# Reordering VectorE's queue around the seam of two Strassen-like stages: an earlier turn of x, earlier sums for C21, and an output addition split by columns

## The chip, the cores and the metric

The kernel runs on one core of a Trainium2 chip. The metric is the device time of one execution in microseconds. The median of three timed runs of the kernel before is 930.23 us (929.91 to 932.08); the profiled execution spans 927.9 us.

## The reference

Shapes are q, k, v: (8, 8, 576, 64), `w_in`: (512, 2048), `w_out`: (2048, 512), `s` and `b`: one number each; all of float32.

```python
kv = np.einsum('bhsd,bhse->bhde', k, v)          # linear attention, no softmax
out = np.einsum('bhsd,bhde->bhse', q, kv)
out = out / np.sqrt(np.mean(out * out, -1, keepdims=True) + 1e-06) * g_norm
x = out.transpose(0, 2, 1, 3).reshape(4608, 512)
h = x @ w_in                                      # (4608, 2048)
g = s * np.maximum(h, 0) ** 2 + b
result = g @ w_out                                # (4608, 512)
```

## The kernel before

**Units.** The 4608 rows are worked off in nine units u = 0 to 8 of 512 rows each. A unit has a first stage, which makes g from x (`mm1...`), and a second, which makes the output from g (`mm2`). While TensorE (PE) works on unit u, the attention of unit u+1 is done beside it in two pairs of row blocks, called A and B: `turn` (transpose of q), `product` (with kv), `back` (transpose back), `square`, `row_sum`, `norm`, `turn_x` (L601, a VectorE transpose of 128x1024 that writes half of the next unit's xT) and `scale`.

**Seven products for eight.** Both stages use Strassen's scheme in Winograd's form: a 2x2 block product is made with seven products, numbered 1 to 7, of sums of blocks. Products 1, 6, 5 and 3 are accumulated one after the other in the same PSUM bank (tag "x"), 7 and 4 in one of tag "y", and 2 has one of tag "z". Between two products the bank is read out to SBUF, by ScalarE (ACT) or VectorE (DVE), and the next product must wait until that is done. In units 2 to 8 the scheme is used at two levels (`mm1_deep`, and `at_two_levels` in `mm2`).

**The first stage of units 2 to 8** is `mm1_deep(u)`. Its `run` (L928) is an order written out by hand: `x1(s)`, `x6(s)`, `y7(s)`, `x5(s)`, `x3(s)`, `y4(s)` are the products of slice s (0 to 3) with what reads them out, and `small(i, pair, m...)` are the products of the second level. `a22(s)` (L844) adds `x5`'s copy to bank y and so frees this bank for `y4(s)`. `done(name, s)` does relu and square on ACT in two activations for each s. The four results in SBUF are g's blocks a11, a12, a21 and a22 ("C21" in the change is the block a21). For the second stage `s1(s)` (a21 + a22) and `s3(s)` (a11 - a21, written over a21) make sums on DVE; `early` makes two 128x512 differences for product 7, and `sums` (`sums_1((5, 6, 3))`) three more for the second stage's first products. Calls `at(n)` in `run` put the attention's steps of the next unit into the order, by the tables in `sides` (L1655): for units 3 to 7 `turn_x` of pair B stands at 17, and for unit 2 `back` of pair B does. `at(15)`, `at(16)`, `at(17)` and `at(18)` follow each other in `run` as its lines show. Unit 8 has no next unit.

**The seam.** The last two products of the first stage, `x3(3)` and `y4(3)`, are run inside the second stage's `rest` (L1376), after its first product `do_1(1)`: `do_1(1)`, `x3(3)`, `y4(3)`, `do_1(2)`, `do_1(6)` and so on.

**The second stage.** For a group of first-level products, `sums_*` makes second-level sums of 128x512 on DVE, `go_*(m)` is the product m on PE, `out_*(m)` reads it out on DVE at L1093, and `do_*` is go and out. The output tile `o` of each half j has four slots of 256 columns. `with_5(j)` adds slot 2 and slot 3 into slot 1, and `with_7(j)` does the like; the products 7 and 3 (`_73`) are read out with slots 2 and 1 as the other operand.

**What sets the order.** Each engine runs its instructions in the order of the program (`manual_schedule`); engines wait for each other by semaphores. Weights for the second stage come from DRAM through a ring of 14 buffers, w_sb, which `pump` fills as products are finished.

Of the kernel before, what the change touches and what calls it, by code (L numbers as in the profile page):

```python
# [16 lines left out]
def kernel(  # L17
# [784 lines left out]
    def mm1_deep(u):  # L802
# [28 lines left out]
        def x6(s):  # L831
            mm1_product(6, u, s, st["x", s], False)
            st["r2", s] = rp.tile([P, 2, TB], FP32, name="r2", tag="ra" if s % 2 else "rb")
            nc.scalar.copy(st["r2", s], st["x", s])
# [17 lines left out]
        def x3(s):  # L852
            mm1_product(3, u, s, st["x", s], False)
            nc.scalar.activation(ga["a21", s], st["x", s], AF.Relu)
            nc.scalar.square(ga["a21", s], ga["a21", s])
# [10 lines left out]
        def s1(s):  # L866
            g_tile("s1", s)
            g_s1(s)
# [55 lines left out]
        def done(name, *steps):  # L924
            for s in steps:
                relu_sq_on_act(ga[name, s])

        def run(at, early, sums):  # L928
            x1(0)
            at(2)  # L930
            x1(1)
            sums_of_x()
            small(2, 0, 1, 2)
            x6(0)
            at(4)
            y7(0)
            small(2, 0, 6, 7)
            at(5)
            x5(0)
            small(2, 0, 5)  # L940
            a22(0)
            at(6)
            x6(1)
            small(2, 0, 3, 4)
            at(7)
            y4(0)
            at(8)
            y7(1)
            done("a11", 0, 1)
            at(9)  # L950
            x5(1)
            a22(1)
            at(10)
            x1(2)
            small(3, 0, 1, 2)
            at(11)
            x1(3)
            y4(1)
            at(12)
            small(3, 0, 6, 7)  # L960
            y7(2)
            at(13)
            small(3, 0, 5)
            x6(2)
            at(14)
            small(3, 0, 3, 4)
            x6(3)
            at(15)
            small(2, 1, 1, 2)
            x5(2)  # L970
            done("a21", 0, 1)
            at(16)
            small(2, 1, 6, 7)
            a22(2)
            y7(3)
            s1(0)
            small(2, 1, 5)
            x3(2)
            small(2, 1, 3, 4)
            s1(1)  # L980
            s3(0)
            s3(1)
            at(17)
            early()
            at(18)
            y4(2)
            done("a11", 2)
            s1(2)
            s3(2)
            x5(3)  # L990
            done("a11", 3)
            a22(3)
            sums()

        last = dict(
            x3=lambda: x3(3), y4=lambda: y4(3), x3_s1=lambda: s1(3), x3_s3=lambda: s3(3),
# [74 lines left out]
    def mm2(u, step=None, side={}):  # L1071
# [288 lines left out]
            (4,), one(lambda j, q: slot(j, 2)[:, q]), one(lambda j, q: slot(j, 2)[:, q])  # L1360
        )

        def with_5(j):

            add(slot(j, 1), slot(j, 2), slot(j, 3))

        def with_7(j):

# [7 lines left out]
        def rest():  # L1376
            do_1(1)
            step["x3"]()
            step["x3_square"]()
            step["y4"]()  # L1380
            do_1(2)
            step["y4_square"]()
            do_1(6)
            step["x3_s1"]()
            go_1(7)
            do_1(5)
            sums_25((5, 6), 2)
            sums_25((7,), 5)
            at(0)
            do_25(1)  # L1390
            do_1(3)
            sums_25((5, 6), 5)
            do_1(4)
            do_25(2)
            at(1)
            step["x3_s3"]()
            s2((0,))
            do_25(6)
            s2((1,))
            sums_25((3,))  # L1400
            go_25(7)
            s2((2,))
            do_25(5)
            s2((3,))
            sums_6(())
            do_6(1)
            sums_6((5, 6))
            at(2)
            do_25(3)
            sums_6((7, 3))  # L1410
            do_25(4)
            if end:
                for j in range(2):
                    store("o1", j, 4 * u + j, left, queues)
            do_6(2, 6)
            s4((0, 1))
            s4((2, 3))
            go_6(7)
            do_6(5)
            sums_73((5, 6), 7)  # L1420
            sums_73((5, 6), 3)
            go_73(1)
            do_6(3)
            with_5(0)
            out_73(1)
            do_6(4)
            with_5(1)
            do_73(2)
            sums_73((7,))
            at(3)  # L1430
            do_73(6)
            sums_73((3,))
            at("sums")
            go_73(7)
            do_73(5)
            sums_4((5, 6))
            do_4(1)
            at(4)
            do_73(3)
            with_7(0)  # L1440
            sums_4((7, 3))
            go_73(4, 7)
            out_73(4, slice(0, 1))
            with_7(1)
            if end:
                for j in range(2):
                    store("o2", j, 4 * u + 2 + j, right, queues)
                store("o1", 0, 4 * u, right, queues)
            else:
                store("o1", 0, 4 * u, queues=queues)  # L1450
            do_4(2, 6)
            go_4(7)
            do_4(5)
            at(5)
            go_73(4, 3)
            out_73(4, slice(1, 2))
            if end:
                store("o1", 1, 4 * u + 1, right, queues)
            else:
                store("o1", 1, 4 * u + 1, queues=queues)  # L1460
            do_4(3)
            at(6)
            if end:
                store("o2", 0, 4 * u + 2, left, queues)
            else:
                store("o2", 0, 4 * u + 2, queues=queues)
            do_4(4)
            if end:
                store("o2", 1, 4 * u + 3, left, queues)
            else:  # L1470
                store("o2", 1, 4 * u + 3, queues=queues)
# [183 lines left out]
    def sides(u, A, B):  # L1655

        first, second = {}, {}
        kv = []  # L1660
        if u in kv_due:
            kv.append(lambda: kv_product(kv_due[u]))
            kv.append(lambda: used(*((u, "kv", (n, m)) for n in range(NP) for m in range(2))))
        q = {half: [partial(loads, u + 2, half)] for half in range(2)}
        if u == 1:
            for s in range(1, NS):
                first[((0, 1), (0, 3), (1, 1))[s - 1]] = list(sums_w_in(s))
            first.update({
                (1, 3): kv,
                (2, 0): [partial(A["turn"], 0), partial(A["turn"], 1)],  # L1670
                (2, 1): [A["product"]],
                (2, 2): [A["back"]],
                (2, 3): [A["square"]],
                (3, 0): [A["row_sum"]],
                (3, 2): [A["norm"], A["turn_x"]],
                (3, 3): [lambda: [load() for load in load_q(12, rest_on=nc.sync)]],
            })
            return first, second
        if u + 1 == U:
            return first, second  # L1680
        if u == 2:
            first = {
                4: [A["turn"]],
                5: kv,
                8: [A["product"]],
                9: [A["back"], B["turn"]],
                10: [A["square"]],
                11: [A["row_sum"]],
                12: [B["product"]],
                13: [A["norm"]],  # L1690
                14: [A["turn_x"]],
                15: q[0],
                17: [B["back"]],
                18: [B["square"]],
            }
            second = {
                0: [B["row_sum"]], 1: [A["scale"]], 2: [B["norm"]], 3: [B["turn_x"], *q[1]],
                "sums": [B["scale"]],
            }
        else:  # L1700
            first = {
                2: [A["turn"]],
                4: [A["product"]],
                5: [A["back"]],
                6: [A["square"], B["turn"]],
                7: [A["row_sum"], *kv],
                8: [A["norm"]],
                9: [A["turn_x"]],
                10: [B["product"], *q[0]],
                11: [B["back"], A["scale"]],  # L1710
                12: [B["square"]],
                13: [B["row_sum"]],
                14: [B["norm"]],
                17: [B["turn_x"], *q[1]],
            }
            second = {1: [B["scale"]]}
        second[5], second[6] = [[lambda n=n: x_sums(u + 1)[n]()] for n in range(2)]
        return first, second

    for u in range(U):  # L1720
# [17 lines left out]
        for s in range(NS if u > 0 else 0):  # L1738
            a = steps[s]

            def at(n):
                for fn in first.get((s, n), []):
                    fn()
# [70 lines left out]
```

## Time and profile before

| what | value |
|---|---|
| time, median of 3 (lowest to highest) | 930.23 us (929.91 to 932.08) |
| span of the profiled execution | 927.9 us |
| PE busy | 904.2 us, 97% |
| PEld (weight loads) busy | 827.0 us, 89% |
| DVE busy | 693.4 us, 75% |
| ACT busy | 255.2 us, 28% |
| DMA | 180.33 MB, mean 194 GB/s |
| one unit, from u=4's `kv_product` (452.34) to u=5's (551.41) | 99.07 us |

Times in a timeline are microseconds from the start of the span. A row gives start, length, engine, line, operation, the tile written and those read, and in brackets the idle time of the engine before the row and what ended it. Successive rows of one engine can overlap by some 0.1 us[...]. In the profile's names, a is any of g's blocks, s the sums of `s1`, sub a second-level sum, r a kept part, o the output tile, sx_ps the bank of the second-level products of the first stage. All matmuls but those of the attention have line 91, additions line 250, subtractions line 253 and scaled read-outs line 1093, since helpers record them.

### The profile page before, as it was taken

The numbers are of one execution on the slowest core, as the hardware profiler recorded it, in microseconds if no ns is written. First come the engines' busy times: TensorE is split into PE (matmuls) and PEld (weight loads), VectorE is DVE, ScalarE is ACT, GpSimd is POOL, SyncE is SP. The second block draws the span as 40 slices with busy tenths as digits, with TensorE's granted clock in tenths as the row PEclk, the third lists the DMA queues.
The fourth block names the chain that finished last, engine by engine and source line by source line (L and its number), as shares of the span: only waits on it lengthen the run. The fifth ranks groups of instructions, "written<-read, shape, count | busy, mean of one in ns | idle before, by whom it ended". The sixth has DMA issues, their size and how long they took to land.

```text
span 927.9 us, 19149 instructions
## 1 busy us (share of the span) xinstructions
PE 904.2 (97%) x7524; PEld 827.0 (89%) x7524; DVE 693.4 (75%) x1259; ACT 255.2 (28%) x463; POOL 224.2 (24%) x418
## 2 busy tenths in 40 slices
PE   7999999999999999999999999999999999999998
PEld 7888888888988998899898988899889988999898
DVE  2889777688568967788668866886779777884686
ACT  3783132211125014410343024401450044102400
POOL 2000017024631333802281027403430300020000
PEclk9999999999999999999999999999999999999999
DMA  9687937249933984389436955496539811891285
GB/s 266 219 299 253 258 99 237 63 133 405 311 108 96 295 278 138 80 260 314 146 83 197 293 159 154 122 307 209 156 84 292 270 41 46 271 299 47 54 250 182
DMA packets 120137, 180.33 MB, mean 194 GB/s; under 512 B 29168, under 2 KB 46320, under 8 KB 120048
## 3 DMA queue, kind: packets, MB, share of 16 engines
q1 hardware_dynamic: 101552, 153.00, 52.8%
q0 software_dynamic: 15040, 23.88, 8.6%
q10 hardware_dynamic: 3456, 2.23, 0.9%
q8 instruction: 60, 0.98, 0.4%
q14 instruction: 29, 0.24, 0.1%
HBM read 153.36 MB, written 25.69 MB: 193 GB/s over the span
## 4 chain that ended last, share of the span: by engine, by line
PE 84%; DVE 13%; DMA 1%; issue 1%; ACT 0%; SPq 0%; DVEq 0%
PE x_ps L91 43%; PE y_ps L91 26%; PE z_ps L91 7%; PE sx_ps L91 4%; DVE a L253 3%; DVE sub L253 2%; PE kv_ps L382 2%; PE y_ps L561 2%; DVE a L250 1%; DMA kv_sb<-in_v_dram 1%; DVE sub L250 1%; DVE s L250 1%; DVE r L1093 1%; DVE o L1093 1%; DVE xT L605 1%
## 5 line engine op out<-in xcount | busy, mean ns | idle before, releaser
L1630 POOL DMA_DIRECT2D q_sb<-in_q_dram x256 | 144.1, 571 | 137.7 <-issue 114.9
L1209 POOL DMA_DIRECT2D out_dram<-o x110 | 55.0, 506 | 418.4 <-DVE o L1093 294.7
L91 PE MATMUL x_ps<-w_sb,sub 128*128 128x128 f32 x1176 | 150.1, 276 | 1.9 <-DVE r L1093 1.9
L91 PEld LDWEIGHTS x_ps<-w_sb,sub 128*128 128x128 f32 x1176 | 139.7, 192 | 4.4 <-DVE r L1093 3.7
L91 PE MATMUL y_ps<-xs,wb 128*128 128x256 f32 x512 | 121.8, 383 | 10.0 <-DVE a L250 10.0
L91 PE MATMUL x_ps<-xs,ws 128*128 128x256 f32 x512 | 121.3, 380 | 0.0
L91 PEld LDWEIGHTS y_ps<-xs,wb 128*128 128x128 f32 x512 | 94.0, 190 | 26.2 <-DVE a L250 12.5
L91 PEld LDWEIGHTS x_ps<-xs,ws 128*128 128x128 f32 x512 | 93.9, 190 | 11.4 <-issue 0.4
L91 PE MATMUL x_ps<-xT,wa 128*128 128x256 f32 x384 | 89.0, 381 | 0.1
L829 ACT COPY a<-x_ps 128x512 f32<-128x512 f32 x28 | 16.4, 586 | 258.3 <-PE x_ps L91 258.3
L250 DVE TENSOR_TENSOR r<-sx_ps,a 128x256 f32<-128x256 f32 x63 | 26.7, 424 | 78.0 <-PE sx_ps L91 77.7
L91 PEld LDWEIGHTS x_ps<-xT,wa 128*128 128x128 f32 x384 | 71.3, 190 | 10.9 <-issue 1.5
L91 PE MATMUL x_ps<-w_sb,a 128*128 128x128 f32 (+1 forms) x432 | 64.9, 298 | 0.0
L91 PE MATMUL y_ps<-w_sb,a 128*128 128x128 f32 (+1 forms) x416 | 62.1, 295 | 0.0
L91 PEld LDWEIGHTS x_ps<-w_sb,a 128*128 128x128 f32 x432 | 59.0, 191 | 3.3 <-issue 0.4
L91 PEld LDWEIGHTS y_ps<-w_sb,a 128*128 128x128 f32 x416 | 56.1, 192 | 2.1
L1093 DVE SCALAR_TENSOR_TENSOR r<-x_ps,s_col,o 128x256 f32<-128x256 f32 (+1 forms) x84 | 34.7, 413 | 29.1 <-PE x_ps L91 28.2
L91 PE MATMUL y_ps<-w_sb,sub 128*128 128x128 f32 x392 | 49.5, 275 | 0.0
L250 DVE TENSOR_TENSOR a<-y_ps,r 128x512 f32<-128x512 f32 x36 | 24.7, 686 | 31.2 <-PE y_ps L91 23.4
L253 DVE TENSOR_TENSOR a<-a,a 128x512 f32<-128x512 f32 x72 | 46.2, 684 | 0.9
L91 PE MATMUL z_ps<-w_sb,a 128*128 128x128 f32 (+1 forms) x352 | 46.8, 280 | 0.0
L91 PEld LDWEIGHTS y_ps<-w_sb,sub 128*128 128x128 f32 x392 | 46.6, 192 | 0.0
(190 smaller groups left out, 1487.3 us busy)
## 6 DMA issues: line engine op xcount, KB each, us to landing
w_sb<-w SPq DMA_DIRECT2D x385, 256.0 KB, 4.4
w_raw<-in_moe_w_in_dram SPq DMA_DIRECT2D x8, 1024.0 KB, 8.0
w_raw<-in_moe_w_out_dram SPq DMA_DIRECT2D x8, 1024.0 KB, 5.0
w_sb<-w SPq DMA_DIRECT2D x14, 512.0 KB, 9.1
w<-sub POOLq DMA_DIRECT2D x28, 256.0 KB, 6.6
w_sb<-in_k_dram SPq DMA_DIRECT2D x24, 288.0 KB, 4.9
w_sb<-in_v_dram SPq DMA_DIRECT2D x24, 288.0 KB, 5.0
out_dram<-o POOLq DMA_DIRECT2D x92, 64.0 KB, 3.7
```

Source lines behind the costliest of these rows:

```text
L91: nc.tensor.matmul(o, lhsT=lhsT, rhs=rhs, start=start, stop=stop, skip_group_check=True)
L250: nc.vector.tensor_tensor(out=o, in0=a, in1=b, op=ALU.add)
L253: nc.vector.tensor_tensor(out=o, in0=a, in1=b, op=ALU.subtract)
L382: nc.tensor.matmul(ps[r][(r ^ l) * HB : (r ^ l) * HB + HB, i, :], lhsT=kv[l][0][rows, j, :], rhs=kv[l][1][rows, j, :], start=(j == 0), sto ...
L561: nc.tensor.matmul(ps[l][32 * p : 32 * p + 32, r, lo:hi], lhsT=bd_kv[b % 2][rows, p, at : at + 32], rhs=st["qT"][rows, p, lo:hi], start=Tr ...
L605: nc.vector.transpose(out=xT[u][:, :, j * P : j * P + 2 * P], in_=st["xn"].rearrange("p (c x) -> p c x", c=KC),)
L829: nc.scalar.copy(g_tile("a11", s), st["x", s])
L1093: nc.vector.scalar_tensor_tensor(o, ps, s_col, other, ALU.mult, ALU.add)
L1209: queues[s % 2].dma_start(out=view[b, jj, :, cols], in_=st[name, j][s * w : s * w + w, cols])
L1630: load()
```

## The change

Three things are moved or split; no matmul changes its place. In `run`, `done("a21", 0, 1)` comes before `at(15)` rather than after `x5(2)`; `s1` and `s3` of slices 0 and 1 are spread between the products from `x5(2)` on, where they stood together after `small(2, 1, 3, 4)`; `s3(2)` comes after `sums`. In `sides`, what stood at 17 (`turn_x` of B with the loads of q, in unit 2 `back` of B) stands at 15. In `rest`, `with_5(0)` is made in two halves of 128 columns, the first ahead of `out_73(1)` and the second after `do_6(3)`, and the second-level sums for product 3 come after these. The aim is that what PE waits for stands nearer to the head of DVE's queue.

```diff
@@ run
             small(3, 0, 3, 4)
             x6(3)
+            done("a21", 0, 1)
             at(15)
             small(2, 1, 1, 2)
             x5(2)
-            done("a21", 0, 1)
+            s1(0)
+            s3(0)
             at(16)
             small(2, 1, 6, 7)
             a22(2)
             y7(3)
-            s1(0)
+            s1(1)
             small(2, 1, 5)
             x3(2)
+            s3(1)
             small(2, 1, 3, 4)
-            s1(1)
-            s3(0)
-            s3(1)
-            at(17)
             early()
             at(18)
             y4(2)
             done("a11", 2)
             s1(2)
-            s3(2)
             x5(3)
             done("a11", 3)
             a22(3)
             sums()
+            s3(2)
@@ mm2
-        def with_5(j):
+        cols = [slice(q * P, q * P + P) for q in range(2)]
 
-            add(slot(j, 1), slot(j, 2), slot(j, 3))
+        def with_5(j, q=slice(0, HN)):
+
+            add(slot(j, 1)[:, q], slot(j, 2)[:, q], slot(j, 3)[:, q])
@@ rest
             do_6(5)
             sums_73((5, 6), 7)
+            sums_73((), 3)
+            go_73(1)
+            with_5(0, cols[0])
+            out_73(1)
+            do_6(3)
+            with_5(0, cols[1])
             sums_73((5, 6), 3)
-            go_73(1)
-            do_6(3)
-            with_5(0)
-            out_73(1)
             do_6(4)
             with_5(1)
@@ sides, u == 2
-                15: q[0],
-                17: [B["back"]],
+                15: [B["back"], *q[0]],
                 18: [B["square"]],
@@ sides, u > 2
-                17: [B["turn_x"], *q[1]],
+                15: [B["turn_x"], *q[1]],
```

`sums_73((), 3)` makes no sum; it only notes the blocks of product 3 that the product 1 reads.

## The prediction

> **What bounds the kernel now.** I read the page's busy table first, then the waits of TensorE, then the timeline of TensorE and VectorE (DVE) around each wait.
>
> ```profile
> PE 904.2 (97%) x7524; PEld 827.0 (89%) x7524; DVE 693.4 (75%) x1259; ACT 255.2 (28%) x463; POOL 224.2 (24%) x418
> ```
>
> TensorE is the bound; all that can be saved without removing a matmul is its idle time. The waits of PE name most of it:
>
> ```profile
> PE y_ps L91 <- DVE a L250: 10.0, 6, 1.8
> PE x_ps L91 <- ACT a L842: 1.9, 1, 1.9
> PE x_ps L91 <- DVE r L1093: 1.9, 7, 0.4
> ```
>
> Seven units, u=2 to 8, run the two functions that the diff touches. The first two lines have seven waits, one a unit; the third has seven more. In the PE timeline of unit u=4 (start us, us, ...) the first kind stands at the seam of the stages:
>
> ```profile
> 486.46 1.05 PE L91 MATMUL x_ps<-w_sb,a 128*128 128x128 f32 x8
> 487.36 1.94 PE L91 MATMUL x_ps<-xT,ws 128*128 128x256 f32 x8
> 491.15 1.99 PE L91 MATMUL y_ps<-xs,wb 128*128 128x256 f32 x8 [1.85 <-DVE a L250]
> 492.98 1.05 PE L91 MATMUL z_ps<-w_sb,a 128*128 128x128 f32 x8
> ```
>
> The rows are the second stage's first product, then `x3(3)`, then `y4(3)`, which accumulates into the bank that `a22(3)` (L846) must have read. What DVE did meanwhile, in its own timeline:
>
> ```profile
> 479.63 0.69 DVE L250 TENSOR_TENSOR s<-a,a 128x512 f32<-128x512 f32 x1
> ...
> 483.55 0.68 DVE L250 TENSOR_TENSOR s<-a,a 128x512 f32<-128x512 f32 x1
> 484.15 1.28 DVE L253 TENSOR_TENSOR a<-a,a 128x512 f32<-128x512 f32 x2
> 485.35 1.24 DVE L605 STREAM_TRANSPOSE xT<-xn 128x1024 f32<-128x1024 f32 x1
> 486.52 1.25 DVE L253 TENSOR_TENSOR sub<-a 128x512 f32<-128x512 f32 x2
> ...
> 489.80 0.69 DVE L253 TENSOR_TENSOR a<-a,a 128x512 f32<-128x512 f32 x1
> 490.41 0.68 DVE L250 TENSOR_TENSOR a<-y_ps,a 128x512 f32<-128x512 f32 x1
> ```
>
> The last row is `a22(3)`. It ends at 491.09 and PE starts at 491.15. Its other input, the ACT copy at L842, ended at 487.26: `a22(3)` waits for its turn in DVE's queue and for nothing else. Ahead of it stand `s1(1)`, `s3(0)`, `s3(1)`, the turn of the second pair's x, and `s3(2)`, which no matmul at the seam needs. The second kind of wait, in PE and then DVE:
>
> ```profile
> 518.88 1.95 PE L91 MATMUL z_ps<-w_sb,a 128*128 128x128 f32 x16
> 521.08 2.05 PE L91 MATMUL x_ps<-w_sb,sub 128*128 128x128 f32 x16 [0.24 <-DVE r L1093]
> 522.97 1.95 PE L91 MATMUL y_ps<-w_sb,sub 128*128 128x128 f32 x16
> ```
>
> ```profile
> 518.37 0.68 DVE L250 TENSOR_TENSOR sub<-a,a 128x512 f32<-128x512 f32 x1
> 519.09 0.69 DVE L253 TENSOR_TENSOR sub<-sub,a 128x512 f32<-128x512 f32 x1
> ...
> 520.08 0.42 DVE L250 TENSOR_TENSOR o<-o 128x256 f32<-128x256 f32 x1
> 520.54 0.48 DVE L1093 SCALAR_TENSOR_TENSOR r<-x_ps,s_col,o 128x256 f32<-128x256 f32 x1
> ...
> 522.05 1.28 DVE L253 TENSOR_TENSOR sub<-a 128x512 f32<-128x512 f32 x2
> ```
>
> `out_73(1)` (the r row) must empty the x bank before `do_73(6)`; it stands behind `with_5(0)` (the o row) and two sums for product 3. DVE is back to back from 513.72 to 524.9.
>
> [...]
>
> **The change part by part.** The matmuls keep their order; ACT, DVE and the number of DVE operations are what changes (one add more a unit).
>
> *First stage, what leaves the queue ahead of `a22(3)`.* In the PE-bound gaps before, DVE stood idle 1.75 us before 475.35, 1.67 before 477.97 and 1.29 before 482.76. The changed order fills them:
> - The turn (1.24 us) goes to 473.6–474.8, its input `xn` being done at 472.85. In u=2 it is `back`'s pair of transposes (1.31 us) instead, from 274.8 to 276.1, before the 276.55 at which the next eviction is due; in u=8 there is neither.
> - On ACT the four activations of `done("a21", 0, 1)` follow the copy that ended at 475.49: 475.4–477.9. Their input, the last small sum, is ready at 473.6. They delay the `x5(2)` copy from 477.52 to about 477.8, so `a22(2)` from 478.31 to 478.4, whose bank PE wants at 483: hidden.
> - `s1(0)` now waits for the first ACT square, about 476.7, and `s3(0)` follows to 478.0. Behind them is `q2`'s eviction, due at 477.97 and needed by PE at 479.94: hidden.
> - `s1(1)` ends about 480.4, before the eviction due at 480.59; `s3(1)` takes 481.4–482.05 in the 1.29 us gap.
> - `early`'s two subs then run 483.55–484.75, the `y4(2)` add when PE is done with it (484.8–485.5), the square to 486.2, `s1(2)` to 486.8. `s3(2)` is behind `sums`.
> - `a22(3)` then starts when ACT's copy ends: 487.3–488.0. PE ends `x3(3)` at 487.36+1.73 = 489.09. The wait is gone with 1.1 us to spare.
>
> *What that is worth.* Without the wait the z row would start at 489.09+1.73 = 490.81; it started at 492.98. So 2.17 us: the 1.85 of idle time and a slower restart. The same row shows 1.85 in u=3 to 7, so 5 x 2.17 = 10.85. In u=2 (the ACT wait; ACT's copy of `x5(3)` stood behind a Square that waited for `back`) the z row would start at 288.55+3.46 = 292.01 and started at 294.24: 2.23. In u=8, 875.81+3.45 = 879.26 against 880.30: 1.04. Sum 14.1 us.
>
> *Does it come back at once?* DVE owes `s3(2)` and three subs after `a22(3)`. The first sub waits for ACT's square of a11(3), 488.44; 0.72+0.72+0.61+0.61 us later, at 491.1, the r1 eviction starts and ends at 491.5. PE wants that bank (`do_1(6)`) at 490.81+0.89 = 491.7. It holds with about 0.2 us. After that DVE again waits for PE, as it did at 494.96 before.
>
> *Second stage.* From 518.37: half an add[...], r at 518.70–519.18 instead of 520.54–521.02, so `do_73(6)` starts on time at 518.88+1.79 = 520.67. Then o 519.10, second half 519.48, the two sums 519.70 and 520.42 (needed by the second half of `do_73(6)` at 521.56, ready 521.1), y's eviction 521.03, `with_5(1)` 521.40, z's 521.75, and the sums for `go_73(7)` at 522.14, 0.09 later than before. PE now comes to `go_73(7)` at 522.46, but its weights are ready only at 522.82. So it starts about 522.88 with the restart's 0.1 us, and the product after it at 524.77, where it was 522.97+1.79 = 524.76. A wait is exchanged for another: 0.0 us. [...]
>
> Sum: 930.2 - 14.1 + 0.0 = 916.1 us.
>
> **The rivals.**
> - *Both waits fall.* Against it: DVE's unbroken row of work up to 522.7. For it: if evictions overlap more than the row's spacing shows, the 522.97-522.46 = 0.51 us of seven units come off too: 916.1-3.6 = 912.5.
> - *The wait moves on.* The 0.2 us at `do_1(6)`, or the ACT square that `s1(0)` now waits for, may be tighter than worked out; a new wait of 1 us in each of seven units leaves 916.1+7 = 923.1. For it: DVE is busy for 8.2 to 9.2 us of each 10 us between 480 and 520. Against it: by the starts above some 2.3 us of DVE gaps are left between 474.8 and 488.5.
> - *Not faster.* If in-order `s1(0)` holds the evictions behind it as long as the old queue did, the seam's gain is given back[...]. Against it: `q2`'s eviction would end at 478.4 and PE wants it at 479.94, so ACT's square would have to come 1.5 us later than the lengths of its rows give.
>
> **How the numbers follow.** Forecast 0.71, both waits 0.12, moved on 0.12, not faster 0.05. The range 912.3 to 920.0 holds the first two with the unknown costs and new waits up to 0.5 us a unit, and leaves out 0.17. Faster by over 0.3% (under 927.4): the first three, 0.95. The last splits into 0.02 within 0.3% and 0.03 slower.
>
> **What would show it.** Right: no wait of PE for `a<-y_ps,a` or the L842 copy; the z row 3.45 us after the x3(3) row's start; the r row about 1.8 us earlier against PE, and a short wait of PE or PEld for `sub` of L253 in place of `r`. Wrong: a wait of PE for an r row of `x_ps` right after the z row, `s1(0)` waiting over 1 us for ACT, or waits for `w_sb` loads, whose landing took 9.2 us at most here.

## The result, and the profile after

The changed kernel takes 917.48 us (median, 917.36 to 917.70) against 930.22 us: a ratio of 0.9859, 95% interval 0.9842 to 0.9876, or 12.7 us less; the ratio and its interval are worked out from all runs, not from the two medians. Measured again in rounds beside the kernel before, it took 916.93 against 931.38 us, ratio 0.9840 (0.9822 to 0.9858). The span of the profiled execution fell from 927.9 to 915.9 us.

From the page's busy table, and from the waits of PE, after:

```profile
PE 903.1 (99%) x7524; PEld 827.9 (90%) x7524; DVE 695.5 (76%) x1266; ACT 254.3 (28%) x463; POOL 223.5 (24%) x418
```

```profile
PE y_ps L91 <- DVE sub L253: 2.3, 7, 0.5
...
PE y_ps L91 <- DVE ss L584: 0.7, 1, 0.7
```

PE's busy time is nearly what it was (904.2 us before); the rest of the span fell from 23.7 to 12.8 us. The three lines of before (`y_ps` for a of L250, `x_ps` for a of L842, `x_ps` for r of L1093) are all gone. Two others have come: seven short waits for a second-level difference, and a single wait of 0.7 us.

The seam in unit 4, in the timeline of PE and then of DVE:

```profile
483.64 1.05 PE L91 MATMUL x_ps<-w_sb,a 128*128 128x128 f32 x8
484.53 1.94 PE L91 MATMUL x_ps<-xT,ws 128*128 128x256 f32 x8
486.31 1.89 PE L91 MATMUL y_ps<-xs,wb 128*128 128x256 f32 x8
488.03 1.05 PE L91 MATMUL z_ps<-w_sb,a 128*128 128x128 f32 x8
```

```profile
470.69 1.23 DVE L605 STREAM_TRANSPOSE xT<-xn 128x1024 f32<-128x1024 f32 x1
...
473.89 0.69 DVE L250 TENSOR_TENSOR s<-a,a 128x512 f32<-128x512 f32 x1 [0.41 <-ACT a L809]
...
484.45 0.69 DVE L250 TENSOR_TENSOR a<-y_ps,a 128x512 f32<-128x512 f32 x1 [0.32 <-ACT a L842]
485.65 0.69 DVE L250 TENSOR_TENSOR sub<-a,a 128x512 f32<-128x512 f32 x1 [0.50 <-ACT a L809]
...
488.31 0.34 DVE L1092 SCALAR_TENSOR_TENSOR r<-x_ps,s_col,b_row 128x128 f32<-128x128 f32 x1
```

The four PE rows follow each other without a bracket. The row of 484.45 is `a22(3)`: DVE has caught up and now waits for ACT's copy, and the bank is free at 485.14, 1.2 us before `y4(3)` starts at 486.31. The turn stands at 470.69, in what was idle time, and `s1(0)` waits 0.41 us for ACT. The r row, which ends at 488.65, is the one that PE wants at 488.92 for `do_1(6)`: the 0.27 us between them is all the room there is.

The second place, PE and then DVE:

```profile
513.94 1.95 PE L91 MATMUL z_ps<-w_sb,a 128*128 128x128 f32 x16
515.72 1.95 PE L91 MATMUL x_ps<-w_sb,sub 128*128 128x128 f32 x16
517.98 2.05 PE L91 MATMUL y_ps<-w_sb,sub 128*128 128x128 f32 x16 [0.31 <-DVE sub L253]
519.87 1.95 PE L91 MATMUL x_ps<-w_sb,sub 128*128 128x128 f32 x16
```

```profile
513.42 0.28 DVE L250 TENSOR_TENSOR o<-o 128x128 f32<-128x128 f32 x1
513.81 0.48 DVE L1092 SCALAR_TENSOR_TENSOR r<-x_ps,s_col,o 128x256 f32<-128x256 f32 x1
...
517.24 1.28 DVE L253 TENSOR_TENSOR sub<-a 128x512 f32<-128x512 f32 x2
```

`do_73(6)` (515.72) starts on time. `go_73(7)` after it waits for the sub row, which DVE reaches only now. From the start of the z row to the start of the last product shown are 5.93 us; before they were 5.87 (518.88 to 524.75).

### The profile page after: what moved, and what is told of

The parts are those of the page before. It is cut to its first block, busy times and chain, and to the rows that moved or that the text cites. A ratio compares the mean times of both kernels' runs of the same rounds, so it can differ in the third digit from the quotient of the medians.

```text
span 915.9 us, 19161 instructions
## 1 busy us (share of the span) xinstructions
PE 903.1 (99%) x7524; PEld 827.9 (90%) x7524; DVE 695.5 (76%) x1266; ACT 254.3 (28%) x463; POOL 223.5 (24%) x418
## 3 DMA queue, kind: packets, MB, share of 16 engines
q10 hardware_dynamic: 3456, 2.23, 1.0%
## 4 chain that ended last, share of the span: by engine, by line
PE 86%; DVE 11%; issue 1%; DMA 1%; ACT 0%; SPq 0%; DVEq 0%
PE x_ps L91 43%; PE y_ps L91 26%; PE z_ps L91 7%; PE sx_ps L91 4%; DVE a L253 2%; PE y_ps L561 2%; DVE sub L253 2%; PE kv_ps L382 2%; DMA kv_sb<-in_v_dram 1%; DVE sub L250 1%; DVE o L1092 1%; DVE b_row L250 1%; DVE r L1092 1%; DVE o L250 1%; DVE w_dn L245 0%
## 5 line engine op out<-in xcount | busy, mean ns | idle before, releaser
L250 DVE TENSOR_TENSOR r<-sx_ps,a 128x256 f32<-128x256 f32 x63 | 26.7, 423 | 59.0 <-PE sx_ps L91 58.9
L250 DVE TENSOR_TENSOR a<-y_ps,r 128x512 f32<-128x512 f32 x36 | 24.8, 688 | 32.3 <-PE y_ps L91 23.8
```

Source lines behind the costliest of these rows:

```text
L250: nc.vector.tensor_tensor(out=o, in0=a, in1=b, op=ALU.add)
```

## Where the time went

From the timelines of PE, the stretch from `x3(2)` to `go_25(7)`, which holds the seam, and the one from there to the next unit's `kv_product`, which holds the second place:

| | before | after | less |
|---|---|---|---|
| seam, unit 2 | 23.37 us | 21.19 us | 2.18 us |
| seam, units 3 to 7, each | 23.30 to 23.31 | 21.18 to 21.19 | 2.11 to 2.12 |
| seam, unit 8 | 22.18 | 21.19 | 0.99 |
| second place, unit 2 | 48.41 | 48.55 | -0.14 |
| second place, unit 3 | 47.65 | 47.71 | -0.06 |

With 2.12 the seams give 2.18 + 5 x 2.12 + 0.99 = 13.8 us, and the second place costs 0.14 + 6 x 0.06 = 0.5 us (units 4 to 8 lose 0.06 us there as unit 3 does). The spans differ by 12.0 us. The rest is two things: the stretch ahead of unit 2's `kv_product`, whose code is the same, was 0.62 us longer in this execution (it starts at 248.07, before at 247.45); and the single wait of 0.67 us for the line "ss" right after unit 4's `kv_product` made its first stage 0.63 us longer. 13.8 - 0.5 - 0.6 - 0.6 = 12.1.

## The experiments

"Before" is the kernel before in the same rounds. In what was expected, A is the account that the prediction rests on, and the rival another that would give other numbers.

| run | time us | before us | ratio (95%) |
|---|---|---|---|
| `after_again` | 916.93 | 931.38 | 0.9840 (0.9822 to 0.9858) |
| `first_only` | 916.41 | 931.38 | 0.9833 (0.9816 to 0.9850) |
| `second_only` | 932.56 | 931.38 | 1.0008 (0.9997 to 1.0018) |
| `sub7_sooner` | 913.34 | 931.38 | 0.9801 (0.9780 to 0.9822) |
| `turn_alone` | 923.43 | 931.71 | 0.9905 (0.9888 to 0.9923) |
| `s3_alone` | 928.06 | 931.71 | 0.9953 (0.9934 to 0.9972) |
| `sums_alone` | 918.31 | 931.71 | 0.9851 (0.9834 to 0.9869) |
| `turn_late` | 917.24 | 931.71 | 0.9843 (0.9822 to 0.9864) |
| `sub7_whole` | 916.08 | 931.23 | 0.9841 (0.9825 to 0.9858) |
| `sub7_turn2` | 912.37 | 931.23 | 0.9800 (0.9785 to 0.9814) |

**Which half of the change carries the gain: `first_only` and `second_only`.** `first_only` is the changed kernel with this put back:

```diff
-            sums_73((), 3)
-            go_73(1)
-            with_5(0, cols[0])
-            out_73(1)
-            do_6(3)
-            with_5(0, cols[1])
             sums_73((5, 6), 3)
+            go_73(1)
+            do_6(3)
+            with_5(0)
+            out_73(1)
             do_6(4)
```

> The first-stage part of the change alone, second stage as before. A (the second-stage split only exchanges one wait for another): 917.0 us, from 916.3 to 917.7; no wait of PE at the seam; in each unit the wait of 0.24 us of x_ps<-w_sb,sub for the r row is back, and that of y_ps<-w_sb,sub for sub is gone. Rival (the split saves the whole of the wait it aims at, 0.5 us a unit): 921 us.

> The second-stage part of the change alone, first stage as before. A: 930.6 us, from 929.9 to 931.3; the seam's waits of 1.85 us stay in units 3 to 7, and PE waits about 0.3 us a unit at y_ps<-w_sb,sub for sub in place of 0.24 at x_ps<-w_sb,sub for r. Rival (the split saves 0.5 us a unit): 926.7 us.

`second_only` is the reverse: the kernel before with the second-stage part alone. The waits of PE, `first_only` and then `second_only`:

```profile
PE x_ps L91 <- DVE r L1092: 1.9, 7, 0.4
```

```profile
PE y_ps L91 <- DVE a L250: 10.0, 6, 1.9
PE y_ps L91 <- DVE sub L253: 2.3, 7, 0.5
PE x_ps L91 <- ACT a L842: 1.9, 1, 1.9
```

`first_only` is inside A's span at 916.41 us, 0.5 us below `after_again`; so the second-stage part does not gain, it costs the 0.5 us of the table above. `second_only` shows the exchange of waits alone: those for r are gone, those for sub are there, those of the seam stay. Its time lies 1.3 us above the end of A's span, and 1.2 us above a before that was itself at 931.38; the ratio's interval holds 1. Its three runs at a mean clock of 0.999 or 1.000 (last section) took 930.41 to 931.19 us, inside A's span. The saving that the rival saw is excluded.

**Is the single wait part of the change: `after_again`.**

> The changed kernel once more. A: PE's wait of 0.67 us in front of y_ps<-xs,wb right after unit 4's kv_product, the only one of its kind in seven units, belongs to that one execution and not to the change; here it is absent, and the span is about 0.7 us shorter. Rival: it is a wait that the change makes (something on DVE or ACT late in unit 4), and it stands at the same place again with 0.5 to 0.8 us. Time 917.0 to 918.0 us.

In this execution 0.12 us of idle time are left at this place (`kv_product` from 448.19 for 2.34 us, the next row at 450.65), the unchanged part ahead of unit 2 takes what it took before (247.45), and the span is 914.9 us, 1.0 us shorter. The time, 916.93 us, is just under the lower end of the span expected. So at least 0.55 of the 0.67 us differ between two executions of the same kernel and do not belong to the change. In other traces unit 4 has 0.26 us there (`turn_alone`, one matmul later) and 0.39 (`sub7_turn2`); before and `first_only` have none. What causes it is open, since DVE's "ss" row, which the trace names, makes nothing that this product reads.

**Which of the moved operations carries the seam: `turn_alone`, `s3_alone`, `sums_alone`, `turn_late`.** The first three make one move each in the kernel before, the fourth takes one move out of the changed kernel:

```diff
@@ turn_alone, from before
-                15: q[0],
-                17: [B["back"]],
+                15: [B["back"], *q[0]],
...
-                17: [B["turn_x"], *q[1]],
+                15: [B["turn_x"], *q[1]],
@@ s3_alone, from before
             s1(2)
-            s3(2)
             x5(3)
...
             sums()
+            s3(2)
@@ sums_alone, from before (the lines put in; they are taken out where they stood)
+            done("a21", 0, 1)
             at(15)
...
+            s1(0)
+            s3(0)
...
+            s1(1)
...
+            s3(1)
@@ turn_late, from the changed kernel
-                15: [B["turn_x"], *q[1]],
+                17: [B["turn_x"], *q[1]],
```

In `turn_late` unit 2's `back` goes back to 17 too, and `at(17)` stands ahead of `early()` again.

> The kernel before with only the turn of the second pair's x (in unit 2: back) moved from 17 to 15. A: one operation of 1.16 us fewer stands ahead of a22(3), so in units 3 to 7 PE's wait at the seam falls from 1.85 to about 0.7 us and the unit gains 1.16; unit 2 loses its wait for the ACT copy and keeps one of 0.85 us, a gain of 1.1; unit 8 has no such operation and gains nothing: 5 x 1.16 + 1.1 = 6.9 us below before. Rival (the turn only fills time that PE's own order sets): no more than 2 us below before.

> The kernel before with only s3(2) moved behind the sums. A: a22(3) comes 0.65 us sooner, but DVE's work up to the r row that frees bank x for do_1(6) is the same, so part of the gain comes back as a new wait of PE there (x_ps<-w_sb,sub for r, 0.2 us and a restart): 0.3 us a unit, about 2 us below before in all. In unit 2 PE's wait is for the ACT copy and stays. Rival (no new wait): 0.65 us in six units, 3.9 us below before.

> The kernel before with only done of a21 and s1, s3 of slices 0 and 1 moved sooner; turn, back and s3(2) as before. A: 1.8 us leave the queue ahead of a22(3); it ends 0.2 us too late for PE, so about 0.5 of the 2.17 us is left in units 3 to 7, 0.5 of 2.23 in unit 2, and nothing in unit 8: 5 x 1.65 + 1.7 + 1.04 = 11.0 us below before. With turn_alone and s3_alone the three parts then add to more than all of them together. Rival (the parts add up): 14 - 6.9 - 2 = 5 us below before.

> The changed kernel with only the turn (in unit 2: back) put back to 17. A: a22(3) then ends 0.6 us ahead of PE, still in time, so units 3 to 8 keep their gain; only unit 2 loses, as back holds up ACT's Square and the copy behind it, by 0.3 to 0.6 us: 917.3 us, from 916.7 to 918.2. Rival (the turn carries its own 1.16 us a unit): 917 + 5 x 1.16 = 922.8 us.

`y4(3)`'s row of unit 4 in the PE timeline of `turn_alone` and of `s3_alone`, and in the weight loads (PEld) of `sums_alone`:

```profile
488.38 1.99 PE L91 MATMUL y_ps<-xs,wb 128*128 128x256 f32 x8 [0.73 <-DVE a L250]
```

```profile
492.13 1.99 PE L91 MATMUL y_ps<-xs,wb 128*128 128x256 f32 x8 [1.05 <-DVE a L250]
```

```profile
486.03 1.59 PEld L91 LDWEIGHTS y_ps<-xs,wb 128*128 128x128 f32 x8 [0.45 <-DVE a L250]
```

The wait shrinks with what was taken out of the queue: from 1.85 to 0.73 us for the turn, to 1.05 for `s3(2)`; with the sums alone the row of PE shows no idle time, and the weight loads a wait of 0.45 us. What each move is worth is read from the stretch from `x3(2)` to `go_25(7)`, as in the table of "Where the time went", which leaves out the scatter of whole runs:

| kernel | unit 2 | units 3 to 7, each | unit 8 | less than before, in all |
|---|---|---|---|---|
| before | 23.37 us | 23.30 to 23.31 us | 22.18 us | |
| `turn_alone` | 22.18 | 22.18 | 22.18 | 6.8 us |
| `s3_alone` | 25.04 | 22.80 to 22.81 | 21.68 | 3.0 us in units 3 to 8 |
| `sums_alone` | 21.57 | 21.50 to 21.51 | 21.19 | 11.8 us |
| `turn_late` | 21.54 | 21.19 | 21.19 | 13.4 us |
| the changed kernel | 21.19 | 21.19 | 21.19 | 13.8 us |

A had 6.9, 2 and 11.0 us for the first three. Unit 2 of `turn_alone` keeps 0.73 us of its wait, where A had 0.85, and unit 8 its 0.72. Unit 2 of `s3_alone` is left out of the sum: its stall of 1.94 us is still there, and a lower clock followed it (0.53 over 3.6 us), which the last section takes up. Whole runs say the same more roughly: against the before of their rounds the three are 8.3, 3.7 and 13.4 us faster, 25.4 us in sum, where the changed kernel gained 14.5 us in its rounds. By the table the three parts come to 21.6 us, and all of them together to 13.8, so they do not add: 2.12 us can be won at a seam of units 3 to 7, and the moves take 0.60 + 1.20 + 1.17 + 0.61 = 3.6 us out of the queue (the distances of the starts of successive rows in DVE's timeline before). So `turn_late`, without the turn's move, is at 917.24 us as A says; `a22(3)` of unit 4 there ends at 485.10, and `y4(3)` starts at 485.74; only unit 2 has its `x3(3)` 0.3 us late (288.94 for 287.75 + 0.89).

`s3_alone` also shows the wait that moves on. The loads of the next product, in PEld of the same unit:

```profile
495.04 0.97 PEld L91 LDWEIGHTS x_ps<-w_sb,sub 128*128 128x128 f32 x8 [0.22 <-DVE r L1093]
```

Counted from the start of `x3(3)`, `y4(3)` comes 0.79 us sooner than before (3.00 us for 3.79), but the r row that frees bank x only 0.19 us (494.64 - 489.13 = 5.51 us for 493.06 - 487.36 = 5.70), since `s3(2)` only changed its place ahead of it. So 0.3 us of this are lost again, and by the table 0.50 us a unit are left: between the 0.3 of A and the 0.65 of the rival. The new wait that A named is there; A's number was too small because `a22(3)` came 0.79 us sooner and not 0.65. Whole runs do not decide between the two: they lie between 926.64 and 929.52 us, and those of before between 931.06 and 935.34.

**Can the second place be won: `sub7_sooner`, `sub7_whole`, `sub7_turn2`.** `sub7_sooner` moves the differences that `go_73(7)` waits for ahead of two operations that PE does not wait for here:

```diff
             do_6(4)
-            with_5(1)
-            do_73(2)
+            go_73(2)
             sums_73((7,))
+            with_5(1)
+            out_73(2)
             at(3)
```

`sub7_whole` does this too, but has the order of before ahead of it (as `first_only`).

> The changed kernel with the two differences for products 7 and 3 of go_73(7) put ahead of with_5(1) and of the read-out of do_73(2). A: what PE waits for at y_ps<-w_sb,sub is only DVE's order; the sub row comes 0.74 us sooner, the wait goes in all seven units, 0.5 us each: 914.0 us, from 913.3 to 914.8. Rival: DVE is full from s4 to there, so the wait moves to the next read-out (r2's bank at go_73(5)), and the time stays at 916.5 to 917.5 us.

> As sub7_sooner, but with the second stage's order of before up to do_6(4): with_5(0) whole and both pairs of sums for product 3 ahead of out_73(1). A (of two waits in a row, the one that comes first sets the time, so taking away the second alone brings nothing): PE waits 0.24 us a unit at x_ps<-w_sb,sub for r, and the time is that of first_only, 916.4 us, from 915.7 to 917.1. Rival (the split of with_5 is not needed): 913.3 us as sub7_sooner.

The PE timeline of `sub7_sooner`, unit 4, and the sub row of DVE:

```profile
514.12 1.95 PE L91 MATMUL x_ps<-w_sb,sub 128*128 128x128 f32 x16
515.91 1.95 PE L91 MATMUL y_ps<-w_sb,sub 128*128 128x128 f32 x16
517.69 1.95 PE L91 MATMUL x_ps<-w_sb,sub 128*128 128x128 f32 x16
```

```profile
514.78 1.28 DVE L253 TENSOR_TENSOR sub<-a 128x512 f32<-128x512 f32 x2
```

No wait is left here: 1.79 us from row to row, and 913.34 us, 3.6 below `after_again` (A had 7 x 0.5). `sub7_whole` stays at 916.08, with PE's seven waits for r (1.9 us in all). So the split of `with_5` is worth nothing while `go_73(7)` waits behind it, and the earlier sums are worth nothing (0.3 us) while `out_73(1)` is late ahead of them; both together are worth 3.1 us against `first_only`.

One wait was left, in the PE timeline of `sub7_sooner`, unit 2:

```profile
324.62 2.05 PE L91 MATMUL x_ps<-w_sb,sub 128*128 128x128 f32 x16 [0.70 <-DVE r L1092]
```

`turn_x` of unit 2's second pair, 1.24 us, stands ahead of this r in the second stage:

```diff
-                0: [B["row_sum"]], 1: [A["scale"]], 2: [B["norm"]], 3: [B["turn_x"], *q[1]],
-                "sums": [B["scale"]],
+                0: [B["row_sum"]], 1: [A["scale"]], 2: [B["norm"]], 3: q[1],
+                "sums": [B["turn_x"], B["scale"]],
```

> As sub7_sooner, with unit 2's turn of the second pair's x put behind go_73(6)'s read-out (from the place 3 of the second stage to the place of the sums). A: the one wait of PE for a VectorE read-out that is left there, 0.70 us of idle time at x_ps<-w_sb,sub in unit 2, goes: 912.5 us, from 911.8 to 913.1. Rival (the wait moves on to a later read-out of unit 2): 913.3 us.

With the turn behind it the wait is gone, and 912.37 us is the lowest time of the study, 0.980 of before.

## Why the prediction was right, and by how much its terms were off

- *The queue ahead of `a22(3)`.* Shown. The trace after has each step where it was put, counted from PE's rows: the turn in the 1.75 us gap, `s1(0)` held by ACT's square for 0.41 us (it was to start at 476.7, and by the clock of before it does at 476.72), `a22(3)` waiting for the ACT copy, 1.2 us to spare (1.1). The partial kernels show that the wait shrinks by what leaves the queue.
- *2.17 us a seam, 14.1 us in all.* The seams gave 2.18, 2.12 and 0.99 us for 2.23, 2.17 and 1.04: 13.8 us. The 0.05 us are the same in each: `y4(3)` starts 1.78 us after `x3(3)` (484.53 to 486.31) and not 1.73, the spacing of the other rows. The row of `x3(3)` was 1.94 us long before, too, where its like are 1.89; the prediction did not use that. What it calls a slower restart are two things in the rows of unit 4: without a wait the rows of `x3(3)` and `y4(3)` overlap by 0.16 us (484.53 + 1.94 - 486.31), and with the wait the row of `y4(3)` is 1.99 us long and the next one starts 1.83 us after it, where after these are 1.89 and 1.72. With the 1.85 us of idle time this gives the 2.12.
- *It does not come back at `do_1(6)`.* Shown in the changed kernel, with 0.27 us to spare for the 0.2 worked out. `s3_alone` shows that this room is real and narrow: there the next wait comes up and takes back 0.3 us.
- *The second stage: 0.0 us.* The exchange of r for sub is as predicted, and the half add takes 0.288 us (mean of 14 rows). No row of before showed its length, on which the prediction's times for this stage rest; a straight line through the rows of before, 0.425 us at 256 columns and 0.685 at 512, gives an estimate of 0.295 at 128. The two halves take 0.15 us more of DVE than the whole add of 0.425. The term was too small: `go_73(7)` and the product after it start 0.04 us later against unit 4's z row than was worked out, and the exchange costs 0.14 us in unit 2 and 0.06 in the others, 0.5 us in all, which the difference of `first_only` and `after_again` gives too.
- *The sum.* 916.1 was said and 917.48 measured. Of the 1.4 us, 0.3 are the seams, 0.5 the second stage, and about 0.6 are in what `after_again`, the same kernel at 916.93 us, did not have. The rivals are out: the wait at `go_73(7)` is there, which "both fall" denied, and PE has no new wait at the seam or at `do_1(6)`, which the other two needed.

## What to carry to other kernels

Here an engine with a quarter of its time idle (DVE, 75% busy) held up the bound engine (PE, 97%) by 1.85 us a seam in units 3 to 7, because operations that nobody needed yet stood in its queue ahead of the one that frees a bank. So look at what lies between the moment at which the operation's inputs are ready and its start (487.26 and 490.41 in unit 4 before), and move that into the gaps before or behind the next read-outs. The removals did not add up (21.6 us one by one, 13.8 together): once the operation waited for its inputs again, or came before it was wanted, more of them brought nothing. Where two waits stand in a row, take away both: here the split addition alone cost 0.5 us and the earlier sums alone brought 0.3, and both together 3.1.

## What was not expected of the hardware

Three of thirteen stalls of about 2 us were followed by a lower granted clock of TensorE, 0.53 to 0.71 over some 3.5 to 4 us, and cost more than their length. In the profile of `second_only` the row after unit 2's stall is 3.60 us long, where it was 1.99 in the profile of before. The row of before, that of `second_only`, and then the windows around it (the stretch and its length; the busy time of PE, PEld, DVE, ACT and POOL with the number of instructions; the granted clock; DMA share and GB/s):

```profile
290.65 1.99 PE L91 MATMUL x_ps<-xT,ws 128*128 128x256 f32 x8 [1.94 <-ACT a L842]
```

```profile
290.40 3.60 PE L91 MATMUL x_ps<-xT,ws 128*128 128x256 f32 x8 [1.94 <-ACT a L842]
```

```profile
280.00:290.00 10.00, 8.46 (x49) 7.52 (x47) 8.38 (x15) 4.96 (x9) 0.58 (x2) 1.00 0.27 72
290.00:294.00 4.00, 3.60 (x9) 2.86 (x10) 3.83 (x7) 3.34 (x7) 0.00 (x0) 0.58 0.18 47
294.00:300.00 6.00, 6.00 (x48) 5.79 (x47) 2.95 (x8) 2.52 (x5) 0.00 (x0) 1.00 0.32 69
```

The clock was 0.58 for these 4 us and 1.00 on both sides. The seam of this unit took 25.03 us where before it took 23.37. The same place in `s3_alone` had 0.53 over 3.6 us, with a row of 3.47 us. The stall of 1.85 us in `second_only`'s unit 7 had 0.71 over 3.5 us and 0.86 over the 5 us after them, with a row of 2.60 us. After the stalls of 1.05 us in `s3_alone` the row is 1.99 us long, as after those of before, and the windows of 3 us at three of them have a clock of 1.00. It did not happen at every stall or in every execution: of the thirteen stalls of 1.85 to 1.94 us in the three traces that have them three were followed by it. The trace of before has six of these, and in it no window of 1 us has a clock under 0.95 but the last one, in which no engine works; in the trace after it is so but for the last two.

The timed runs fit this. Each has a mean clock, and one such stretch, 4 us at 0.58 in 930 us, takes 0.002 off it, by estimate: the profiled run of `s3_alone` with one has 0.998, that of `second_only` with two 0.996. Of the 31 runs of before in the later rounds ten have 1.000 and took 929.36 to 931.34 us, sixteen have 0.997 or 0.998 and took 931.21 to 932.32, and five have 0.995 or 0.996 and took 932.91 to 935.34. The 36 runs of the nine kernels without a stall of over 1 us in units 2 to 8 all have 0.999 or 1.000. So by estimate the change gains twice: from the median of those ten runs, 930.4 us, to `after_again`'s 916.93 are 13.5 us, close to the 13.3 that the traces give (13.8 - 0.5), and the other 1.0 of the 14.5 us would be time that the kernel before lost to the clock. Where in these runs the clock fell was not traced, and why it follows some stalls and not others is open.
